# Two heads of a pair on even and odd partitions, and 128 neighbouring tokens per tile in the last mixture

## The chip, the cores and the metric

One core of one Trainium2 chip. The metric is the device time of one execution in microseconds. TensorE is PE here (its weight loads PEld), VectorE DVE, ScalarE ACT, GpSimd POOL; SyncE (SP) issues most DMAs.

## What is computed

Three stages in float32, each on the output of the one before:

```python
# attention: 4 batches x 8 heads x 576 tokens x 64; heads 0..3: the 32 tokens up to the query,
# heads 4..7: every fourth of the 128 tokens up to the query
scores = where(masks, scale * q @ k.T, -1e9)
attn = softmax(scores) @ v                            # x: 2304 tokens x 512
# soft mixture: 8 experts x 4 slots
logits = x @ phi                                      # phi 512 x 32
slots = softmax(logits, axis=0).T @ x                 # 32 x 512
so[e] = relu(slots[e] @ w1[e]) @ w2[e]                # 512 -> 1024 -> 512
x = softmax(logits, axis=1) @ so
# last mixture: 8 experts, each token to the best by cosine, times its probability
e = argmax(cosine(x, emb) / tau);  gate = softmax(...)[e]
out = gate * relu(x @ w1b[e]) @ w2b[e]
```

## The kernel before

Lines are those of the kernel as printed below and in the profile.

**Attention.** The work goes by supercolumns: a pair of heads in two batches, 8 of them, each three score tiles, so 24 tiles numbered n. A tile holds 128 queries' blocks in three columns z. The keys of the pair lie in `kbd`, a block-diagonal tile: head 0's 64 dimensions on partitions 0 to 63 in one half of the columns, head 1's on 64 to 127 in the other half, and zeros elsewhere, so that one product gives both heads' scores. Values (`v1`) lie the same way, their second half in the rows of the second head; `v2` is a copy of `v1` shifted by half a block. `load_kq` (L135) and `load_v` (L142) issue the loads on SP, two for keys, one for queries, two for values; the zeros are written once by `zero` (L148), of which the loads touch nothing.

A loop with an order written by hand runs a pipeline over n: `emit_soft` (DVE's maximum L242 and subtract L244), `emit_S` of the next tile (PE L231, 24 products, and the mask as one more, L234), `emit_T` (PE L255, ACT copy L257), `emit_XT`, `emit_exp` (ACT L249), `emit_PV` (PE L267, DVE L271 to 273), `emit_v2` once per supercolumn (DVE and POOL copies L211 and 212, ACT copy L214), and `emit_logits` (PE L304) once per supercolumn. The product of the scores reads the keys so (partitions; then head, half, 32 neighbouring keys):

```python
k = bass.AP(tensor=flat.tensor, offset=flat.offset + S * bb + 32 * (t // 2),
            ap=[flat.ap[0], [2 * S, 2], [gap, 2], [1, 32]])
```

The logits of pairs 0 and 1 of a batch group read neighbouring columns of x; those of pairs 2 and 3 (dilated heads, stored by residue) read columns 144 apart. The loads of the next supercolumn and the first weights of the experts, `load_w`, are issued from within the loop, in SP's order.

**Soft mixture.** 32 weight tiles of 1 MB are streamed through buffers that become free as attention ends; PE does two layers per expert. `combine_a` (L370) turns the logits by tokens into 18 groups `lt`, 16 of them 64 tokens from each of two places, the last two what is left.

**Last mixture (the tail).** The kernel takes the expert of the first token for all (`w1b`, `w2b` of that expert are loaded early) and treats other tokens in a conditional part that this input doesn't enter. It uses that relu(h) is h or 0: the columns of the hidden layer whose sign is the same for all tokens are taken as linear (`B4`), and only the others are done per token.

- `part_a` (L838), `fold_a` (L844): slots times the first weights, split into a high and a low part, A4; `sign` (L884) the sign for the first token.
- `seen` (L907): for each of 8 blocks of 128 hidden units, products of A4 with all tokens (PE L917, L912) and a reading of them: relu with a sum over the columns, on DVE (L925) or ACT (L923) in turn, 896 or 512 columns at a time.
- `places` (L952): the units that change sign get a place among the "uncertain" ones, by counting; `select` (L971): a one-hot matrix, 128 columns on DVE, a second one of 256 on POOL; `names` (L984): the units' row numbers and the gather of their second weights `w2g` (POOL L990); `gathered` (L993), `hidden` (L1005), `split_w` (L1014): their first weights, their activations as high and low part, and their second weights as the same. A first set of up to 128 units, those that change sign anywhere behind the first 512 tokens of the order, is done for all tokens; a second of up to 256, which change only among those 512, for them alone.
- `route_a` to `route_h`: cosine, argmax and gate. `root` (L177) makes the square roots for it, on POOL, behind the second select.
- `through` (L1018): four products per output tile (L1021, 1024 to 1026), ten for a tile of the first 512 tokens; `put` (L849) the gate, on ACT (L852) or DVE (L854), and the store (L864).

```python
select(nc.gpsimd, 1)
split_w(0)
route_d()
route_e()        # the root, on POOL
```

Of the kernel before, what the change touches and what calls it, by code (L numbers as in the profile page):

```python
# [16 lines left out]
NSET = 2  # L17

def layout(q, k, v):
# [44 lines left out]
def body(ctx, tc, a, stop=None):  # L64
# [156 lines left out]
    def emit_S(n):  # L221
        sc, p, kb, si, t0 = tiles(n)
        s = ps.tile([128, 3, 2, 64], F32, tag="s", name="s")
        flat = kbd[si].rearrange("d h b s -> d (h b s)")
        for z in range(3):
            for i, (bb, t) in enumerate(ublocks(t0 + z)):
# [3 lines left out]
                            ap=[flat.ap[0], [2 * S, 2], [gap, 2], [1, 32]])  # L230
# [4 lines left out]
            s, lhsT=identb, rhs=maskb[:, p // 2, t0:t0 + 3, None, :].to_broadcast([128, 3, 2, 64]),  # L235
# [134 lines left out]
    def combine_a(kb):  # L370

        r = slice(64 * kb, 64 * kb + 64)
        tp = ps.tile([128, 4, 64], F32, tag="t", name="tm")
        for m in range(4):
            nc.tensor.transpose(tp[:, m], Lsb[r, 128 * m:128 * m + 128], ident[r, r])
        sp = ps.tile([128, 32], F32, tag="v", name="ts")
        for hh in range(2):
            nc.tensor.matmul(sp[64 * hh:64 * hh + 64], lhsT=Lsb[r, 512:576], rhs=ident[r, 64 * kb + 32 * hh:64 * kb + 32 * hh + 32], start=True, stop=True)

        o = lt[:, 0:16].rearrange("p (m k b) s -> p k m b s", k=2, b=2)[:, kb]  # L380
        nc.scalar.copy(out=o, in_=tp.rearrange("p m (b s) -> p m b s", b=2))
        nc.scalar.copy(out=lt[:, 16 + kb], in_=sp)
# [81 lines left out]
    def keep_warm(n):  # L464
# [10 lines left out]
    keep_warm(4)  # L475
# [9 lines left out]
    keep_warm(2)  # L485
# [755 lines left out]
```

## Time and profile before

| | us |
|---|---|
| median of three runs (lowest, highest) | 245.94 (244.4, 247.26) |
| the profiled execution | 248.36 |
| its span, first to last instruction | 246.6 |
| PE busy | 197.7 (80%) |
| DVE busy | 127.6 (52%) |
| ACT busy | 103.6 (42%) |
| DMA queue 1, share of 16 engines' span | 73.3% |

Shares are means over three stages with different limits, so the slices and the stretches come first. The mean granted clock of PE over the span is 0.942. All durations below come from the profiled execution. In a row of the timeline, the first number is the start in the span, the second the time from the first start to the last end of what the row groups, and the bracket is the engine's idle time before it with what ended it.

### The profile page before, as it was taken

The numbers are of one execution on the slowest core, as the hardware profiler recorded it, in microseconds if no ns is written. First come the engines' busy times: TensorE is split into PE (matmuls) and PEld (weight loads), VectorE is DVE, ScalarE is ACT, GpSimd is POOL, SyncE is SP. The second block draws the span as 40 slices with busy tenths as digits, with TensorE's granted clock in tenths as the row PEclk, the third lists the DMA queues.
The fourth block names the chain that finished last, engine by engine and source line by source line (L and its number), as shares of the span: only waits on it lengthen the run. The fifth ranks groups of instructions, "written<-read, shape, count | busy, mean of one in ns | idle before, by whom it ended". The sixth has DMA issues, their size and how long they took to land. (4 is left out here: it accounts for less than half of the span.)

```text
span 246.6 us, 5616 instructions
## 1 busy us (share of the span) xinstructions
PE 197.7 (80%) x2206; PEld 128.4 (52%) x2206; DVE 127.6 (52%) x362; ACT 103.6 (42%) x226; POOL 42.3 (17%) x89
## 2 busy tenths in 40 slices
PE   1549779887959795999999999888699479489970
PEld 1227556655637574545543434555565457457860
DVE  6525856646494737545244123535886642636720
ACT  2142748646567736435332124424567040134210
POOL 8522010202020202120000130000020098400000
PEclk9999999999999999999999999999999755589996
DMA  5999999999999999999999999398000010045742
GB/s 162 238 234 267 299 234 279 269 315 293 293 289 234 348 264 373 334 353 390 385 386 387 387 385 386 94 338 321 1 1 0 0 45 0 17 153 213 248 141 93
DMA packets 27745, 58.25 MB, mean 236 GB/s; under 512 B 2048, under 2 KB 4480, under 8 KB 27712
## 3 DMA queue, kind: packets, MB, share of 16 engines
q1 hardware_dynamic: 27472, 57.04, 73.3%
q0 software_dynamic: 240, 0.79, 1.2%
q8 instruction: 19, 0.31, 0.6%
q14 instruction: 14, 0.11, 0.2%
HBM read 53.10 MB, written 4.72 MB: 234 GB/s over the span
## 5 line engine op out<-in xcount | busy, mean ns | idle before, releaser
L231 PE MATMUL s<-kbd,qt 128*32 128x128 f32 x576 | 27.0, 305 | 23.1 <-DMA qt<-in_q 12.9
L231 PEld LDWEIGHTS s<-kbd,qt 128*32 128x32 f32 x576 | 18.6, 121 | 31.8 <-issue 14.4
L257 ACT COPY et<-tp 128x384 f32<-128x384 f32 x24 | 11.5, 479 | 27.9 <-PE tp L255 27.9
L267 PE MATMUL pv<-v,et 128*32 128x130 f32 x576 | 21.9, 284 | 0.0
L211 POOL COPY v<-v 32x1040 f32<-32x1040 f32 x8 | 8.4, 1052 | 75.2 <-DMA v<-in_v 75.2
L249 ACT ACTIVATE e<-e 128x384 f32<-128x384 f32 x24 | 12.7, 528 | 19.6 <-DVE e L244 19.4
L214 ACT COPY v<-v 32x1170 f32<-32x1170 f32 x16 | 18.5, 1158 | 1.2 <-DMA v<-in_v 1.0
L540 ACT COPY hs<-hp 128x512 f32<-128x512 f32 x16 | 9.2, 584 | 20.2 <-PE hp L539 20.2
L267 PEld LDWEIGHTS pv<-v,et 128*32 128x32 f32 x576 | 15.0, 110 | 4.3 <-issue 4.2
L244 DVE TENSOR_TENSOR e<-s,mx 128x384 f32<-128x384 f32 x24 | 13.4, 558 | 2.3
L273 DVE TENSOR_TENSOR x<-pv,rd 128x384 f32<-128x384 f32 x24 | 13.4, 558 | 0.8
L304 PE MATMUL L<-xT,phi 128*32 128x288 f32 x64 | 13.7, 539 | 0.0
L242 DVE TENSOR_REDUCE mx<-s 128x6 f32<-128x384 f32 x24 | 13.2, 550 | 0.8 <-PE s L234 0.6
L925 DVE TENSOR_SCALAR_CACHE_REDUCE junk<-H,ms 128x896 bf16<-128x896 f32 (+1 forms) x12 | 12.2, 1015 | 2.7 <-PE H L917 1.9
L539 PE MATMUL hp<-w,siT 128*32 128x512 f32 x104 | 13.1, 597 | 0.0
L923 ACT ACTIVATE junk<-H,ms 128x896 bf16<-128x896 f32 (+1 forms) x12 | 10.8, 900 | 5.3 <-PE H L917 3.0
L211 DVE COPY v<-v 32x1040 f32<-32x1040 f32 x8 | 5.5, 693 | 14.3 <-DMA v<-in_v 14.2
L255 PE MATMUL tp<-cst,e 128*128 128x128 f32 x72 | 12.6, 287 | 0.4 <-ACT e L249 0.4
L559 PE MATMUL so_p<-w,h 128*32 128x512 f32 x102 | 12.5, 595 | 0.3 <-DVE h L551 0.2
L281 PE MATMUL xp<-cst,x 128*128 128x128 f32 x72 | 12.0, 276 | 0.8 <-ACT dn L355 0.4
L852 ACT ACTIVATE hs<-y,gm 128x512 f32<-128x512 f32 x9 | 6.2, 689 | 14.6 <-DVE hs L854 8.1
L549 DVE TENSOR_REDUCE hr<-hTp 128x16 f32<-128x64 f32 x16 | 3.6, 222 | 16.3 <-PE hTp L547 16.3
(291 smaller groups left out, 382.6 us busy)
## 6 DMA issues: line engine op xcount, KB each, us to landing
w<-in_w1a SPq DMA_DIRECT2D x12, 1024.0 KB, 13.4
w<-in_w2a SPq DMA_DIRECT2D x12, 1024.0 KB, 11.3
v<-in_v SPq DMA_DIRECT2D x16, 292.5 KB, 7.0
out<-hs SPq DMA_DIRECT2D x16, 256.0 KB, 2.2
kbd<-in_k SPq DMA_DIRECT2D x14, 288.0 KB, 8.3
qt<-in_q SPq DMA_DIRECT2D x7, 576.0 KB, 9.3
wG<-in_w2a SPq DMA_DIRECT2D x3, 1024.0 KB, 11.8
wG<-in_w1a SPq DMA_DIRECT2D x3, 1024.0 KB, 11.6
```

What stands on the lines that cost most here:

```text
L211: cp(out=d_[o0:o1, hh, :, 1:9], in_=s_[o0:o1, hh, :, 0:8])
L214: nc.scalar.copy(out=d_[e0:o0, hh], in_=s_[e0:o0, hh])
L231: nc.tensor.matmul(s[32 * i:32 * i + 32, z], lhsT=qt[si][:, bb, 32 * t:32 * t + 32], rhs=k, start=(z == 0), stop=False, skip_group_check=True)
L242: nc.vector.tensor_reduce(out=mx, in_=s, axis=AX.X, op=ALU.max)
L244: nc.vector.tensor_tensor(out=e, in0=s, in1=mx[:, :, :, None].to_broadcast([128, 3, 2, 64]), op=ALU.subtract)
L249: nc.scalar.activation(out=e, in_=e, func=AF.Exp, scale=0.125)
L255: nc.tensor.transpose(tp[:, z], e[:, z].rearrange("q h c -> q (h c)"), ident)
L267: nc.tensor.matmul(pv[32 * i:32 * i + 32, z], lhsT=et[:, z, 32 * i:32 * i + 32], rhs=vt[:, :, bb, t // 2, :], start=True, stop=True)
L273: nc.vector.tensor_tensor(out=x[kb][p // 2][:, p % 2, t0:t0 + 3, :].rearrange("q z (h d) -> q z h d", h=2), in0=pv[:, :, :, 0:64], in1=rd. ...
L304: nc.tensor.matmul(st["L"][n][r0:r0 + 32], lhsT=phi[:, p, :], rhs=rhs, start=(p == 0), stop=(p == 3))
L539: nc.tensor.matmul(hp[32 * c:32 * c + 32], lhsT=siT[:, c, :], rhs=w_t[4 * e + n][:, c], start=True, stop=True)
L559: nc.tensor.matmul(so_p[32 * j:32 * j + 32], lhsT=h[:, f, :], rhs=w_t[4 * e + 2 + f // 4][:, j], start=(e == 0 and f < 4), stop=(e == 6 an ...
```

## The change

1. *Layout and loads.* Head hh of a pair stands on partitions hh, hh + 2, hh + 4, ...; loads of keys and values go to 64 partitions with a step of two. Queries are loaded before keys. The tiles are zeroed whole, ahead of the loads. The score's columns are (key, head) instead of (head, key), so that the transposed scores come out on the partitions on which the values lie.
2. *Token groups.* Groups 0 and 1 hold the first 64 tokens of each batch, every further group 128 neighbours. 256 instead of 512 tokens pass the 256 further units.
3. *Tail.* Readings of 1,024 columns with a written engine each; places, select and hidden of the first set ahead of the last readings (256 columns each); the root ahead of gather and second select on POOL; a tile's linear product last; one store for two tiles.

```diff
+        nc.sync.dma_start(out=qt[i][:, bs], in_=a["q"][p, kb, :, bs])
         for hh in range(2):
-            nc.sync.dma_start(out=kbd[i][64 * hh:64 * hh + 64, hh, bs], in_=a["k"][p, kb, 64 * hh:64 * hh + 64, bs])
-        nc.sync.dma_start(out=qt[i][:, bs], in_=a["q"][p, kb, :, bs])
+            nc.sync.dma_start(out=kbd[i][hh:128:2, hh, bs], in_=a["k"][p, kb, 64 * hh:64 * hh + 64, bs])
...
-            nc.sync.dma_start(out=v1[i][64 * hh:64 * hh + 64, hh, bs], in_=a["v"][p, kb, 64 * hh:64 * hh + 64, bs])
-
-    def zero(eng, t):
-
-        eng.memset(t[0:64, 1], 0.0)
-        eng.memset(t[64:128, 0], 0.0)
+            nc.sync.dma_start(out=v1[i][hh:128:2, hh, bs], in_=a["v"][p, kb, 64 * hh:64 * hh + 64, bs])
+    nc.vector.memset(kbd[0][:, 0, 0], 0.0)
+    nc.gpsimd.memset(kbd[0][:, 1, 0], 0.0)
+    nc.vector.memset(kbd[0][:, :, 1], 0.0)
+    nc.gpsimd.memset(v1[0][:, 0], 0.0)
+    nc.vector.memset(v1[0][:, 1], 0.0)
+    for i in range(1, NSET):
+        for hh in range(2):
+            nc.gpsimd.memset(kbd[i][:, hh], 0.0)
+        for hh in range(2):
+            nc.gpsimd.memset(v1[i][:, hh], 0.0)
     load_kq(0, slice(0, 1))
...
-                cp(out=d_[o0:o1, hh, :, 1:9], in_=s_[o0:o1, hh, :, 0:8])
+                cp(out=d_[64:128, hh, :, 1:9], in_=s_[64:128, hh, :, 0:8])
...
-        s = ps.tile([128, 3, 2, 64], F32, tag="s", name="s")
+        s = ps.tile([128, 3, 64, 2], F32, tag="s", name="s")
...
-                            ap=[flat.ap[0], [2 * S, 2], [gap, 2], [1, 32]])
+                            ap=[flat.ap[0], [gap, 2], [1, 32], [2 * S, 2]])
...
-        nc.vector.tensor_reduce(out=mx, in_=s, axis=AX.X, op=ALU.max)
+        nc.vector.tensor_reduce(out=mx, in_=s.rearrange("p z c h -> p z h c"), axis=AX.X, op=ALU.max)
...
-    nc.vector.tensor_copy(out=soTx[:, :, 32:128], in_=sT[:, :, 32:128])
+    nc.scalar.copy(out=soTx[:, :, 32:128], in_=sT[:, :, 32:128])
...
+    def put_pair(p, y, eng):
+        ob = obs[p % 3]
+        for i, g in enumerate(pair(p)):
+            gated(ob[:, i], y[:, 512 * i:512 * i + 512], eng, gm[:, g:g + 1])
+        r0 = S * (2 * (p // 4) + p % 2) + 64 + 256 * (p % 4 // 2)
+        nc.sync.dma_start(out=a["out"][r0:r0 + 256].rearrange("(i t) f -> t i f", i=2), in_=ob)
...
+    def seen(j, part, eng):
+
         H = two("H")
...
+        for i in range(2):
+            nc.tensor.matmul(H[:, 512 * i:512 * i + 512], lhsT=A4[:, 128 * j:128 * j + 128],
+                             rhs=cTf[:, 256 + 1024 * part + 512 * i:768 + 1024 * part + 512 * i], start=True, stop=True)
+        reading(eng, j, part, H, 1024)
...
+        if n == 0:
+            nc.vector.tensor_tensor(out=sel[0][:, 4 * h:4 * h + 4], in0=iota1[:, None, 0:128].to_broadcast([128, 4, 128]),
+                                    in1=pos[0][:, 4 * h:4 * h + 4].to_broadcast([128, 4, 128]), op=ALU.is_equal)
...
+    for q in range(4):
+        part_a(q)
+    for q in range(4):
+        fold_a(q)
...
+    seen(5, 1, D_)
+    route_d()
+    seen(6, 0, A_)
+    seen(6, 1, D_)
+    seen(7, 0, A_)
+    seen(7, 1, D_)
+    H0 = [first64s(0)]
...
+    places_a(0)
+    pp = places_b(0)
+    total(0, pp)
+    seen0(0, H0[0], A_)
+    H0.append(first64s(1))
+    bf = linear_fold()
+    select(0, 0)
+    select(0, 1)
+    names(0, sel[0])
+    gathered(0, sel[0])
+    seen0(1, H0[1], D_)
+    hps = [two("hp") for _ in range(2)]
+    for i in range(4):
+        products(hps[i // 2][:, 512 * (i % 2):512 * (i % 2) + 512], 0, 256 + 512 * i, 512)
+    places_a(1)
+    pp = places_b(1)
...
+        rest(src, Rh[:, r], Rl[:, r])
+        if i == 1:
+            split_hi(0)
+            split_lo(0)
+        if i == 0:
+            split_rows(B4, bf)
+    select(1, 0)
+    select(1, 1)
+    route_f()
+    route_h()
...
+    tiles2(0, 8)
+    tiles2(1)
+    puts(0, A_)
```

`route_d` now sums the logits (DVE) and makes the root (POOL); `first64s` makes four products of 256 columns, `seen0` reads them; `tiles2(0, 8)` does eight products of the identity with itself (`keep_warm`) before its own, in the buffer that these then overwrite.

SP's queue at the start, the loads of the first supercolumn. Before:

```order
L139 DMA kbd_96<-in_k 64x576 x2
L140 DMA qt_97<-in_q 128x576
L155 DMA cst<-in_cst 128x168
L156 DMA x_92<-in_cst 128x320
L139 DMA kbd_96<-in_k 64x576 x2
L140 DMA qt_97<-in_q 128x576
L146 DMA v_0_98<-in_v 64x1170 [waits DMAHW0_49]
```

and now, where `DVE_49` and `Pool_49` are the zeroing:

```order
L139 DMA qt_97<-in_q 128x576
L141 DMA kbd_96<-in_k 64x576 [waits DVE_49]
L141 DMA kbd_96<-in_k 64x576 [waits Pool_49]
L162 DMA cst<-in_cst 128x168
L163 DMA x_92<-in_cst 128x320
L139 DMA qt_97<-in_q 128x576
L141 DMA kbd_96<-in_k 64x576 [waits DVE_49]
```

The queries moved to the front, and the keys wait for zeros.

POOL in the tail, from the first gather on (w2g), with the select (sel) and the start of the root (n, rn, nr). Before:

```order
L990 DMA w2g_2184<-in_w2b,ids_2181 128x512
L973 TENSOR_SCALAR sel_2180<-iota_1912,pos 128x256 x8
L181 TENSOR_SCALAR n_2148<-n_2148 128x18
L182 TENSOR_SCALAR rn<-n_2148 128x18
L185 TENSOR_TENSOR nr_2469<-rn 128x18
```

and now, from the root's last two operations on:

```order
L188 TENSOR_TENSOR rn<-rn,nr_2343 128x18
L189 TENSOR_TENSOR rn<-rn,n_2143 128x18
L1001 DMA w2g_2184<-in_w2b,ids_2181 128x512
L982 TENSOR_SCALAR sel_2179<-iota_1907,pos_2174 128x256 x8
L1001 DMA w2g_2185<-in_w2b,ids_2182 128x512
```

The root moved from behind gather and select to ahead of both.

PE in the tail, from the last readings' products (H) to the names of the first set (ip) and their first weights (am). Before:

```order
L917 MATMUL H<-cT_1908,A_2157 128x448 x4
L912 MATMUL H<-cT_1908,A_2157 128x512
L941 MATMUL Bf<-bs,foldw 128x512
L960 LDWEIGHTS before
L960 MATMUL pp<-flb,before 128x16
L961 LDWEIGHTS every
L961 MATMUL pp<-flb,every 128x16
L962 LDWEIGHTS every
L962 MATMUL pp<-flb,every 128x16
L988 MATMUL ip<-fid,sel_2179 128x2 x8
L998 MATMUL am<-sel_2179,AT_2168 128x128 x8
```

and now:

```order
L917 MATMUL H<-cT_1903,A_2152 128x512 x12
L925 MATMUL H_2375<-cT_1903,A_2152 128x256 x4
L939 MATMUL Bp<-w2b_2049,ATl 32x512 x4
L939 MATMUL Bp<-w2b_2050,ATl 32x512 x4
L965 LDWEIGHTS before
L965 MATMUL pp<-flb_2169,before 128x8
L966 LDWEIGHTS every
L966 MATMUL pp<-cum_2171,every 128x8
L967 LDWEIGHTS every
L967 MATMUL pp<-flb_2169,every 128x8
L925 MATMUL H_2402<-cT_1903,A_2152 128x256 x4
L945 MATMUL Bf<-bs,foldw 128x512
```

The linear part (Bp, Bf) and the small readings moved between the last large readings and the names, which follow next.

## Rows read from the trace of the kernel before

**Rows 1.** The page's slices: granted clock in tenths, and GB/s

```profile
PEclk9999999999999999999999999999999755589996
...
GB/s 162 238 234 267 299 234 279 269 315 293 293 289 234 348 264 373 334 353 390 385 386 387 387 385 386 94 338 321 1 1 0 0 45 0 17 153 213 248 141 93
```

**Rows 2.** Stretches: us; busy (count) of each engine, clock, DMA share, GB/s

```profile
core 0: us, PE busy (x) PEld busy (x) DVE busy (x) ACT busy (x) POOL busy (x), PEclk, DMA share, GB/s
...
14.60:18.40 3.80, 0.22 (x2) 0.00 (x0) 0.00 (x0) 2.06 (x3) 0.00 (x0) 1.00 1.06 240
30.00:36.00 6.00, 5.17 (x98) 3.82 (x94) 2.79 (x7) 2.31 (x6) 0.01 (x1) 1.00 0.99 234
...
120.00:150.00 30.00, 29.59 (x267) 11.75 (x259) 9.41 (x38) 8.95 (x18) 3.82 (x13) 1.00 1.05 387
...
190.50:194.00 3.50, 0.54 (x4) 0.21 (x3) 2.16 (x11) 1.16 (x3) 0.00 (x0) 0.99 0.00 0
194.00:218.00 24.00, 18.20 (x61) 15.19 (x62) 10.11 (x31) 4.26 (x8) 14.15 (x26) 0.50 0.14 41
```

**Rows 3.** The page's DMA issues: count, KB each, us to landing

```profile
v<-in_v SPq DMA_DIRECT2D x16, 292.5 KB, 7.0
...
kbd<-in_k SPq DMA_DIRECT2D x14, 288.0 KB, 8.3
```

**Rows 4.** Waits: us in total, times, longest

```profile
DVE v L211 <- DMA v<-in_v: 14.2, 7, 3.0
PE s L231 <- DMA qt<-in_q: 12.9, 6, 5.2
```

**Rows 5.** Timeline of PE: the starts of score tiles 3, 8, 9 and 23

```profile
18.44 0.87 PE L231 MATMUL s<-kbd,qt 128*32 128x128 f32 x12 [3.62 <-DMA qt<-in_q]
...
36.72 0.86 PE L231 MATMUL s<-kbd,qt 128*32 128x128 f32 x24 [1.55 <-DVE e L244]
...
39.78 0.86 PE L231 MATMUL s<-kbd,qt 128*32 128x128 f32 x24 [0.46 <-DMA qt<-in_q]
...
95.59 0.86 PE L231 MATMUL s<-kbd,qt 128*32 128x128 f32 x24 [2.26 <-DVE e L244]
```

**Rows 6.** Line 304, 36 to 46 and 46 to 58 us: ns min/median/max, starts

```profile
L304 PE MATMUL L<-xT,phi x8: 403/405/406, 42.2 to 42.9; 128*32 128x288 f32 x8
...
L304 PE MATMUL L<-xT,phi x8: 648/670/679, 52.6 to 54.1; 128*32 128x288 f32 x8
```

**Rows 7.** Timeline of DVE at the start

```profile
1.02 1.02 DVE L150 MEMSET kbd<- 64x1152 f32 x1 [1.02 <-PEq L1231]
```

**Rows 8.** Line 925, DVE's readings: ns min/median/max, first and last start

```profile
L925 DVE TENSOR_SCALAR_CACHE_REDUCE junk<-H,ms x12: 749/1142/1151, 171.3 to 189.7; 128x896 bf16<-128x896 f32 x8, 128x512 bf16<-128x512 f32 x4
```

**Rows 9.** Timeline of the tail

```profile
192.41 0.17 DVE L953 TENSOR_TENSOR fl<-acc 128x8 f32<-128x8 f32 x1
...
197.03 1.19 POOL L990 DMA_INDIRECT w2g<-in_w2b,ids  x1 [13.94 <-DVE ids L989]
198.27 7.65 POOL L973 TENSOR_SCALAR sel<-iota,pos 128x256 fp32r<-128x256 f32 x8
...
202.23 0.80 PE L1021 MATMUL y<-B,cT 128*128 128x512 f32 x1 [1.31 <-DVE Rl L1003]
...
206.59 3.41 PE L988 MATMUL ip<-fid,sel 128*128 128x2 f32 x16
...
210.52 0.18 DVE L192 TENSOR_SCALAR rn<-rn 128x18 f32<-128x18 f32 x1 [5.62 <-POOL rn L189]
...
213.10 2.07 PE L998 MATMUL am<-sel,AT 128*128 128x256 f32 x8 [3.10 <-DVE ids L989]
...
213.93 0.24 DVE L801 SCALAR_TENSOR_TENSOR gm<-idm,e0b,gate 128x18 f32<-128x18 f32 x1
...
219.96 0.50 PE L1021 MATMUL y<-B,cT 128*128 128x512 f32 x1 [1.18 <-DVE Sl L1003]
...
238.77 0.39 PE L1026 MATMUL y<-Wl,Sh 128*128 128x512 f32 x1
...
240.03 0.69 ACT L852 ACTIVATE hs<-y,gm 128x512 f32<-128x512 f32 x1 [3.86 <-DVE hs L854]
```

More of the change, by code (lines that the diff above doesn't have):

```diff
@@ L877, in body @@
     nc.gpsimd.memset(acc, 0.0)
[L878 removed]
+    junk = {e: late.tile([128, 1024], BF16, name=f"junk{i}") for i, e in enumerate((nc.scalar, nc.vector))}
     wq = lambda i, name, dt=F32R: wA.tile([128, 4, 512], dt, tag=f"w{i}", name=name)
@@ new lines, in body, with places_a @@
+    cum = [late.tile([128, 8], BF16, name=f"cum{i}") for i in range(2)]
+    pos = [late.tile([128, 8, 1], F32, name=f"pos{i}") for i in range(2)]
+    n12 = late.tile([128, 2], F32, name="n12")
+    for t in flb:
+        nc.gpsimd.memset(t, 0.0)
+    def places_a(n):
+        if n == 0:
+            nc.vector.scalar_tensor_tensor(out=flb[0][:, 1:9], in0=acc[:, 0], scalar=-1.0, in1=acc[:, 1], op0=ALU.mult, op1=ALU.is_lt)
+        else:
+            nc.vector.scalar_tensor_tensor(out=flb[1][:, 1:9], in0=acc[:, 2], scalar=0.0, in1=flb[0][:, 1:9], op0=ALU.is_gt, op1=ALU.is_gt)
+        nc.vector.tensor_tensor_scan(out=cum[n], data0=every[:, 0:8], data1=flb[n][:, 0:8], initial=0.0, op0=ALU.mult, op1=ALU.add)
@@ L1060, in body @@
-    linear_part()
-    for p in range(3):
-        seen(6, p)
+    seen(4, 1, A_)
     route_b(1)
+    seen(5, 0, A_)
     route_c(1)
-    for p in range(3):
-        seen(7, p)
-    linear_fold()
-    places()
-    select(nc.vector, 0)
+    seen(5, 1, D_)
[5 more added lines that the diff above has]
+    H0 = [first64s(0)]
+    bp = one("Bp")
+    linear_part(0, bp)
+    linear_part(1, bp)
+    places_a(0)
+    pp = places_b(0)
+    total(0, pp)
@@ new lines, in body, with tiles2, puts @@
+    select(1, 0)
+    select(1, 1)
+    route_f()
+    route_h()
+    ys = {}
+    def tiles2(p, warm=0):
+        y = ys[p] = two("y")
+        keep_warm(warm, y[:, 0:512])
+        for i, g in enumerate(pair(p)):
+            r = slice(128 * (g - 2), 128 * (g - 2) + 128)
+            through(y[:, 512 * i:512 * i + 512], 0, Rh[:, r], Rl[:, r], first=True)
+            linear(y[:, 512 * i:512 * i + 512], g)
+    def puts(p, eng):
+        put_pair(p, ys.pop(p), eng)
+    tiles2(0, 8)
+    tiles2(1)
@@ new lines, in body @@
+    route_y()
+    tiles2(3)
+    route_z(one("sm"))
+    n3 = late.tile([128, 4], F32, name="n3")
+    gt8 = late.tile([128, 8], F32, name="gt8")
+    nc.vector.tensor_scalar(out=n3[:, 0:1], in0=n12[:, 0:1], scalar1=128.0, scalar2=0.0, op0=ALU.subtract, op1=ALU.max)
+    nc.vector.tensor_scalar(out=n3[:, 1:2], in0=n12[:, 1:2], scalar1=256.0, scalar2=0.0, op0=ALU.subtract, op1=ALU.max)
+    nc.vector.tensor_tensor(out=n3[:, 2:3], in0=n3[:, 0:1], in1=n3[:, 1:2], op=ALU.add)
+    nc.vector.tensor_scalar(out=gt8, in0=iota8, scalar1=8.0, scalar2=128.0, op0=ALU.add, op1=ALU.mult)
@@ new lines, in body @@
+    for k in (1, 2):
+        products(hp[:, 256 * k - 256:256 * k], k, 0, 256)
+    rest(hp, Sh[:, 256:768], Sl[:, 256:768])
+    puts(3, A_)
+    tiles2(5)
+    puts(4, D_)
+    split_hi(1)
+    split_lo(1)
+    split_hi(2)
+    split_lo(2)
+    tiles2(6)
+    puts(5, A_)
+    tiles2(7)
+    puts(6, D_)
+    ys0 = [one(f"ys{g}") for g in range(2)]
+    for g in range(2):
+        for k in range(3):
+            c = 256 * k + 128 * g
+            through(ys0[g], k, Sh[:, c:c + 128], Sl[:, c:c + 128], first=(k == 0))
+        linear(ys0[g], g)
+        if g == 0:
+            puts(7, A_)
+        put(g, ys0[g], (D_, A_)[g], obs[2][:, g], gm)
@@ L1160, in body @@
+        with tc.For_i(0, more, 1):
+            for h in range(2):
+                select(0, h)
+            nc.vector.tensor_scalar(out=pos[0], in0=pos[0], scalar1=-128.0, scalar2=None, op0=ALU.add)
             names(0, sel[0])
             gathered(0, sel[0])
-            hidden(0, 512, 1024, Rh[:, 0:1024], Rl[:, 0:1024])
-            hidden(0, 1536, 768, Rh[:, 1024:1792], Rl[:, 1024:1792])
-            hidden(0, 0, 512, Sh[:, 0], Sl[:, 0])
-            split_w(0)
+            for i in range(5):
+                c0, n = (0, 256) if i == 4 else (256 + 512 * i, 512)
+                hp = one("hp")[:, 0:n]
+                products(hp, 0, c0, n)
+                r = slice(512 * i, 512 * i + 512) if i < 4 else slice(0, 256)
+                rest(hp, (Rh if i < 4 else Sh)[:, r], (Rl if i < 4 else Sl)[:, r])
+            split_hi(0)
+            split_lo(0)
```

373 lines of the change are left out of this document (138 added, 235 removed).

## The prediction

> **What bounds the kernel now.** I read the page's slices first. They show three stages: to about 107 us (slice 17) most slices carry 231 to 330 GB/s; to about 154 us they carry 385 GB/s; behind that almost nothing until the outputs, and the clock row falls to 7, 5, 5, 5, 8 from 191 us on [rows 1]. The table of stretches adds what the slices hide: in the first stage the DMA engines are busy all the time too, 234 GB/s at a share of 0.99 in a stretch of keys and values against 387 GB/s at 1.05 in the weights' stretch [rows 2]. So that stage fills its DMA time without moving what those engines can move. Keys and values are what it moves in pieces over 64 neighbouring partitions: 14 x 288 KB, 4 halves of that for the first pair, and 16 x 292.5 KB of values [rows 3], 9.5 MB; at 234 GB/s they take 40.6 us, at 387 they would take 24.6.
>
> Then who waits: PE starts scores late for queries 12.9 us in all, and DVE its copy of the values 14.2 [rows 4]; the subtract that PE needs is queued behind that copy, so the second wait comes back at PE as 1.55 and 2.26 us behind DVE [rows 5]. From the start of score tile 3 at 18.44 to that of tile 23 at 95.59 it takes 77.15 us for 20 tiles, 3.86 a tile; tiles 8 and 9 stand 3.06 apart, with 0.46 of waiting in it [rows 5]. Over those 20 tiles I count 13.4 us of PE waiting ahead of scores, most of it one step or two behind a load, so the work without it takes 63.8.
>
> In the middle stage the weights are late. The first that fills it is issued in mid-attention, so it ends a fixed time behind attention. In the tail, readings of the expert's first product alternate on DVE and ACT (DVE: 1.142 us for 896 columns, 12 readings to 190.8 [rows 8]); then comes a chain: places at 192.41, gather at 197.03, first output product at 202.23. POOL selects from 198.27 for 7.65 us, and only then makes the root, which DVE takes at 210.52; the gates that every output waits for are there at 213.93 + 0.24. From 219.96 to 238.77 PE makes 80 products back to back, 79 steps of 0.238; the last gating ends at 240.72, the span at 246.6, 5.9 later [rows 9].
>
> **The change, part by part.** *Loads.* The same bytes go to every second partition over the whole height. At the rate of full-height loads keys and values lose 40.6 - 24.6 = 16 us of DMA time, loads are no longer late, and the 13.4 us of PE waiting go; tile 3 could start when PE is free, 3.62 us sooner [rows 5]. The bound below is no gain: the rate stays at 234. I take the full rate, the row of the loads that reach all heights.
>
> [...]
>
> *Zeroing.* Whole tiles are zeroed ahead of the loads: the first key loads wait for a memset of 576 columns on DVE and one on POOL. One of 1152 columns took 1.02 us [rows 7]; half of it, 0.5, is late at the start, and queued behind the waiting key load on SP are the constants and all that follows. POOL's others add up to some 8 us and end before their loads' turn at SP; if not, tile 3 gives back up to 1 us. Three pieces on v2 go.
>
> *Scores.* The two heads alternate in the column order, so PE reads consecutive columns of keys 4,608 bytes apart. No row shows this read. The nearest is the logits product: 405 ns (median) with its columns side by side, 670 with columns 576 bytes apart [rows 6]; by its starts a pair of them takes 242 ns in the one case and some 490 in the other, twice the time. A score tile has six groups of four products, 109 ns each by their starts (0.86 us for the 24 with the last one's tail [rows 5]): doubled, +0.65 us a tile, +15.7 over 24 tiles. The bound below is 0, if two interleaved runs of neighbours read like one. The bound above: the 490 ns are two slow reads that share one limit; then the 24 products of a tile go one by one at 109 ns, 2.6 us instead of 0.8. I take the middle, as the nearest row has it: while strided logits ran, score products in the other column groups kept their pace, which speaks against a shared limit.
>
> [...]
>
> *Sum for attention.* Tile 3 at 18.44 - 3.62 + 0.5 = 15.3, 3.1 sooner; from there to tile 23 63.8 + 20 x 0.65 = 76.8 against 77.15, 0.3 sooner. So PE gives back nearly all that the loads free. Another 2.0 come as the last values, ahead of the weights in SP's queue, move 585 KB faster (1.0) and a backlog of about 1 us goes. The weights' stretch ends 5.5 earlier. DVE's reduce now steps by two elements in PSUM, and the v2 copies cover 64 partitions with the same count and free size: I cost both at nothing, as PE's 3.1 a tile covers DVE; if they took half as long again they would cost some 1 us a tile, and DVE would be late.
>
> *Tail.* Of the readings 16 of 1,024 and 8 of 256 columns are left, the small ones behind the first places. DVE did 8 large (1.142) and 4 small (0.749), 12.1 us [rows 8]; now 7 x 1.28 = 9.0 (128 columns more, by the slope between its two forms, 0.13): -3.1. Between its last reading and the places lay the split of B, 1.6 us, which moves behind: -1.5. The four groups of the first product now stand in a row ahead of the readings: -1.3, an estimate. Places at 192.4 - 5.9 = 186.5. Select in two operations on DVE instead of eight: -0.6; the gather goes at 190.4 (197.03), the first output product at 197.2 with 1.6 for the hidden parts in four pieces (5.2 behind the gather before).
>
> The root stands ahead of gather and select on POOL, and its 4.6 us (205.92 to 210.52) run beside the readings. What is late for the gates now is DVE, with the pieces to about 198.5 and the route's 3.65 behind them: 202.1 instead of 214.17. Three y buffers hold 24 products, 5.7 us, so PE hardly stops: 84 products (12 fewer, as 256 instead of 512 tokens pass three times) x 0.238 = 20.0 from 197.2, with names (3.41) and gather (2.07) of the second set 5.5 [rows 9]: 222.7, last gating 223.4 against 240.72: -17.3. I take -15.5, leaving 1.8 for waits that I can't see. One store for two tiles: the last stores are as small as before: 0.
>
> *The clock.* [...] If the drop comes again, 18.2 us of PE work at the half level cost some 9 more than at full. Eight warming products now stand ahead of the first outputs. I take no drop, at 6 in 10.
>
> *Total.* The profiled execution took 248.36 (span 246.6): 248.4 - 5.5 - 15.5 = 227.4. It lies 2.4 above the runs' median of 245.94; 225.0.
>
> **The rivals.** *P0, the strided read is free*: two runs of neighbours alternate, and each line may still be at hand. Attention gains the 13 us that PE gives back in the forecast: 225 - 13 = 212; 221 with the drop. Against it: 670 ns. *P2, slow reads share one limit* (the slower side): place, the 24 products of each score tile; price 1.8 x 20 = 36 us, less 13.4 of waiting that is gone, less 3.3 at the start: +19.3; 245.9 + 19.3 - 15.5 = 249.7, 258.7 with the drop. It decides from about 2.4 us a score tile on (0.8 now). Against it: the pace of scores beside strided logits. *L, the loads don't speed up*: the waits stay, and PE's 0.65 a tile falls partly into them, +5: 245.9 + 5 - 15.5 = 235.4, 244.4 with the drop.
>
> **How the numbers follow.** The forecast has 0.62: 225 without the drop, 234 with it; its own range is 219 to 236. P0 0.20, L 0.10, P2 0.08. The range of 207 to 241 holds the forecast, P0 and most of L, and leaves out P2 and far ends. A measurement of this kernel tells 1% (2.5 us) from no change. Faster by more: forecast, P0, most of L, 0.89; within it L with the drop, 0.03; slower P2, 0.08.
>
> **What would show it.** Score products: a tile's 24 in 0.8 us (P0), 1.45 (forecast) or over 2.4 (P2). DVE's 14.2 us of waiting for values near 0, and GB/s near 380 while keys and values load (L: below 260). Tail: root ahead of the select, gates at least 9 us sooner behind the first reading than before, the clock row at 0.5 or not. I am wrong if tile 3 to tile 23 takes under 70 or over 82 us, or if first reading to last gating shrinks by less than 10.

## The result, and the profile after

| | us |
|---|---|
| before, median | 246.18 (244.4 to 247.26, 4 runs) |
| after, median | 218.84 (218.52 to 220.04, 4 runs) |
| ratio | 0.8905, 95% interval 0.8842 to 0.8968 |
| profiled execution: span before, after | 246.6, 216.8 |

Some executions of a kernel are slower as a whole, by more than 1.5% over its fastest; the ratios, and the medians below, leave these out. A later comparison gave 218.30 and a ratio of 0.8764 (0.8709 to 0.8820). The forecast was 225.0 in 207 to 241. The forecast's own range was 219 to 236, so the kernel came out just under its lower end, about midway between the forecast and the 212 of rival P0.

The span is 29.8 us shorter. Three starts divide it: DVE's first copy of the slots' outputs (soTx), with which the tail begins, the last gating on ACT, and the end. From the start to soTx: 164.86 before, 153.70 now, -11.2. From there to the end of the last gating: 75.9 before, 58.2 now (211.86), -17.7. From there to the end: 5.9, now 4.9, -0.9. The first of these starts, before and now:

```profile
164.86 0.29 DVE L729 COPY soTx<-sT 128x128 f32<-128x128 f32 x1 [2.07 <-PE sT L722]
```

```profile
153.70 0.29 DVE L727 COPY soTx<-sT 128x128 f32<-128x128 f32 x1 [2.07 <-PE sT L719]
```

The page's slices of the changed kernel (5.42 us each here), to be read against [rows 1]:

```profile
PEclk9987999999999999999999999999999999999996
...
GB/s 147 296 328 384 219 302 313 319 397 374 255 297 306 379 322 302 334 391 387 386 387 385 387 388 386 386 177 204 357 216 0 0 2 51 1 41 249 302 299 90
```

The dip of the clock in the tail is gone; there is a new, short one in the third and fourth slice. In the first stage 13 of 16 slices carry 296 GB/s or more, where before most stood under 300; the fastest slices of either kernel hold weights too. The weights' plateau ends at 141 us (slice 26) instead of 154. Stretches, in the columns of [rows 2]; at 9 to 13 us almost only keys, queries and values are loaded:

```profile
9.00:11.00 2.00, 2.00 (x34) 1.17 (x30) 1.42 (x3) 1.02 (x2) 0.00 (x0) 1.00 1.02 348
11.00:13.00 2.00, 1.56 (x25) 0.98 (x16) 1.44 (x4) 1.04 (x3) 1.06 (x2) 1.00 0.94 356
...
14.00:24.00 10.00, 8.44 (x145) 6.31 (x149) 6.16 (x18) 4.21 (x8) 1.29 (x2) 0.83 0.96 352
24.00:30.00 6.00, 6.00 (x122) 4.55 (x119) 4.86 (x11) 3.65 (x10) 1.20 (x2) 1.00 0.64 189
```

The same 9 to 13 us carried 226 and 265 GB/s before. The packets in the trace show it load by load. The 1,024 packets of 4,680 bytes, a size that only the values have, took 321 ns (median) before and take 181 now; all their bytes over all their time on 16 engines are 228 and 346 GB/s. At 24 to 30 us the DMA engines are busy 0.64 only while PE is busy all the time: attention now waits for PE there, not for loads. The DMA issues and the wait that answer to [rows 3] and [rows 4]:

```profile
v<-in_v SPq DMA_DIRECT2D x16, 292.5 KB, 4.1
...
kbd<-in_k SPq DMA_DIRECT2D x14, 288.0 KB, 6.8
```

```profile
PE s L230 <- DMA kbd<-in_k: 9.4, 4, 5.2
```

Values land in 4.1 instead of 7.0 us, and DVE's wait for them (14.2) is no longer among the large ones. Of PE's 9.4, 5.2 is the start of the kernel, as in the 12.9 before. Score tiles 3, 8, 9 and 23, as in [rows 5]:

```profile
14.89 1.41 PE L230 MATMUL s<-kbd,qt 128*32 128x128 f32 x24 [2.33 <-DMA kbd<-in_k]
...
31.36 1.02 PE L230 MATMUL s<-kbd,qt 128*32 128x128 f32 x24 [0.56 <-DVE e L243]
33.93 1.00 PE L230 MATMUL s<-kbd,qt 128*32 128x128 f32 x24
...
83.20 1.02 PE L230 MATMUL s<-kbd,qt 128*32 128x128 f32 x24
```

From tile 3 to tile 23 it is 68.31 us (77.15). PE is busy 64.9 us of it and stands 3.4, before 63.7 and 13.5. A tile's 24 products take 1.00 us where they took 0.86, so the alternating read costs 0.14 us a tile. (A row counts both passes of a product: the 24 are 12 calls in the code.) Tile 3's 1.41 us is another matter, taken up at the end. DVE's readings and the tail, as in [rows 8] and [rows 9]:

```profile
L911 DVE TENSOR_SCALAR_CACHE_REDUCE junk<-H,ms x11: 473/1276/1283, 161.5 to 182.3; 128x1024 bf16<-128x1024 f32 x7, 128x256 bf16<-128x256 f32 x4
```

```profile
175.91 0.17 DVE L958 SCALAR_TENSOR_TENSOR flb<-acc 128x8 bf16<-128x8 f32 x1
...
177.56 0.23 POOL L189 TENSOR_TENSOR rn<-rn,n 128x18 f32<-128x18 f32 x1
...
181.09 1.19 POOL L1001 DMA_INDIRECT w2g<-in_w2b,ids  x1 [3.30 <-DVE ids L1000]
...
184.01 7.61 POOL L982 TENSOR_SCALAR sel<-iota,pos 128x256 fp32r<-128x256 f32 x8 [1.73 <-DVE n L973]
...
185.76 0.50 PE L1030 MATMUL y<-Wh,Rh 128*128 128x512 f32 x1 [0.32 <-ACT Wh L1020]
...
192.00 0.24 DVE L795 SCALAR_TENSOR_TENSOR gm<-idm,e0b,gate 128x18 f32<-128x18 f32 x1
...
211.17 0.69 ACT L846 ACTIVATE ob<-ys,gm 128x512 f32<-128x512 f32 x1 [3.36 <-PE ys L1026]
```

Counted from soTx (153.70 here, 164.86 before): places at 22.2 (27.5), gather at 27.4 (32.2), first output product at 32.1 (37.4), gates at 38.3 (49.1), last gating's start at 57.5 (75.2). The root ends (177.79) before the select has begun.

### The profile page after: what moved, and what is told of

Its sections match the earlier page's. It is cut to its first block, busy times and chain, and to the rows that moved or that the text cites. A ratio compares the mean times of both kernels' runs of the same rounds, so it can differ in the third digit from the quotient of the medians.

```text
span 216.8 us, 5600 instructions
## 1 busy us (share of the span) xinstructions
PE 190.0 (88%) x2213; PEld 122.1 (56%) x2213; DVE 124.5 (57%) x344; ACT 103.8 (48%) x232; POOL 40.4 (19%) x90
## 4 chain that ended last, share of the span: by engine, by line
PE 58%; DVE 15%; DMA 11%; ACT 6%; issue 4%; SPq 3%; POOL 1%; DVEq 0%; ACTq 0%; POOLq 0%
DMA kbd<-in_k 10%; PE so_p L556 6%; PE hp L536 6%; PE pv L266 5%; PE s L230 5%; PE L L303 3%; PE hTp L544 3%; PE xp L280 2%; PE tp L254 2%; PE si_p L364 2%; PE y L1032 2%; PE H L917 2%; PE y L1030 2%; PE y L1026 1%; PE s L233 1%
## 5 line engine op out<-in xcount | busy, mean ns | idle before, releaser
L230 PE MATMUL s<-kbd,qt 128*32 128x128 f32 x576 | 29.4, 319 | 10.7 <-DMA kbd<-in_k 9.4
L230 PEld LDWEIGHTS s<-kbd,qt 128*32 128x32 f32 x576 | 20.3, 117 | 17.4 <-issue 5.2
L210 POOL COPY v<-v 64x1040 f32<-64x1040 f32 x8 | 9.0, 1127 | 64.2 <-DMA v<-in_v 58.8
L213 ACT COPY v<-v 64x1170 f32<-64x1170 f32 x16 | 18.5, 1158 | 0.0
L248 ACT ACTIVATE e<-e 128x384 f32<-128x384 f32 x24 | 12.9, 536 | 11.4 <-DVE e L243 11.4
L243 DVE TENSOR_TENSOR e<-s,mx 128x384 f32<-128x384 f32 x24 | 13.4, 558 | 2.7 <-ACT et L256 0.5
L909 ACT ACTIVATE junk<-H,ms 128x1024 bf16<-128x1024 f32 (+1 forms) x13 | 11.9, 918 | 4.4 <-PE H L917 4.1
L272 DVE TENSOR_TENSOR x<-pv,rd 128x384 f32<-128x384 f32 x24 | 13.4, 558 | 0.8
L270 DVE TENSOR_SCALAR rd<-pv 128x6 f32<-128x6 f32 x24 | 3.9, 163 | 15.0 <-PE pv L266 14.5
L911 DVE TENSOR_SCALAR_CACHE_REDUCE junk<-H,ms 128x1024 bf16<-128x1024 f32 (+1 forms) x11 | 10.9, 989 | 0.7 <-PE H L917 0.5
L254 PEld LDWEIGHTS tp<-cst,e 128*128 128x128 f32 x72 | 9.5, 145 | 2.1 <-issue 1.0
```

The costliest lines, as they stand in the source:

```text
L213: nc.scalar.copy(out=d_[0:64, hh], in_=s_[0:64, hh])
L230: nc.tensor.matmul(s[32 * i:32 * i + 32, z], lhsT=qt[si][:, bb, 32 * t:32 * t + 32], rhs=k, start=(z == 0), stop=False, skip_group_check=True)
L243: nc.vector.tensor_tensor(out=e, in0=s, in1=mx[:, :, None, :].to_broadcast([128, 3, 64, 2]), op=ALU.subtract)
L248: nc.scalar.activation(out=e, in_=e, func=AF.Exp, scale=0.125)
L254: nc.tensor.transpose(tp[:, z], e[:, z].rearrange("q c h -> q (c h)"), ident)
L272: nc.vector.tensor_tensor(out=x[kb][p // 2][:, p % 2, t0:t0 + 3, :].rearrange("q z (h d) -> q z h d", h=2), in0=pv[:, :, :, 0:64], in1=rd. ...
```

## The experiments

Kernels that were compared together share their runs of the kernel before; its median was 246.4 us beside the first four below, 247.1 beside the next four and 248.4 beside the last three, with a spread of some 3 us. So the ratios and the profiles carry more than differences of medians, and a difference of 1 or 2 us between kernels of two comparisons tells nothing.

**The read of the keys, undone.** Score columns side by side, and DVE's subtract makes the alternation:

```diff
-                            ap=[flat.ap[0], [gap, 2], [1, 32], [2 * S, 2]])
+                            ap=[flat.ap[0], [2 * S, 2], [gap, 2], [1, 32]])
...
-        nc.vector.tensor_tensor(out=e, in0=s, in1=mx[:, :, None, :].to_broadcast([128, 3, 64, 2]), op=ALU.subtract)
+        nc.vector.tensor_tensor(out=e.rearrange("p z c h -> p z h c"), in0=s, in1=mx[:, :, :, None].to_broadcast([128, 3, 2, 64]), op=ALU.subtract)
```

> The changed kernel, but the scores' columns are again (head, key), read side by side, and DVE's subtract writes them in the order (key, head). Theory A (two alternating runs of neighbours read almost like one): a tile's 24 score products go back from 1.00 us, first start to last end, to 0.86; 24 tiles x 0.14 = 3.4 us of PE, so 215.4 to 218 us. Rival B (the forecast's price of 0.65 a tile is there and shows elsewhere on PE): at least 10 us less, under 209. Rival C (PE isn't what attention waits for any more): 218.8, no change, though the products are shorter.

Measured: 216.92 us (215.98 to 217.52), ratio 0.8811 (0.8724 to 0.8899). PE's timeline of this kernel:

```profile
29.60 0.86 PE L230 MATMUL s<-kbd,qt 128*32 128x128 f32 x24
```

The products are back at 0.86, as theory A has it, and soTx comes at 151.54 instead of 153.70. Rival B is out: no 10 us are hidden there. That DVE writes by twos costs it nothing (562 ns a subtract against 558, means of line 243).

**What a read costs.** Spare products behind attention, 24 calls per kind, twice as many as in a score tile, reading a weight tile that has landed, for example

```diff
+    for _ in range(6):
+        for i in range(4):
+            nc.tensor.matmul(wt[32 * i:32 * i + 32, 0:128], lhsT=phi[:, i], rhs=reads((1, 32), (144, 4)), start=True, stop=True)
```

> The changed kernel, with spare products behind attention, into a buffer that nothing reads: per kind of read of the moving operand 24 products of 128 columns over four column groups, as in a score tile; kinds: side by side; 2 runs 4,608 bytes apart, alternating; 3 runs; 4 runs 576 bytes apart (the order of the dilated logits); one run with steps of 8, 16 and 60 bytes; and side by side and 4 runs on one column group alone. Theory A (what counts is how many lines are alternated between or left at once): 2 runs take some 1.2 times side by side, 4 runs 2 times, steps of 8 bytes little, 16 and 60 bytes 2 times. Rival B (each jump to another line costs the same): 2 runs cost as much as 4 runs, 2 times. Rival D (a limit shared by column groups): the four-run read on one column group alone is no slower than side by side on one group, and slow only when four groups run. The kernel itself gets longer by the products, some 10 to 14 us; that is no result.

One execution, 236.53 us. PE's timeline; the lines are, in this order, side by side, 2 runs, 4 runs, 3 runs (126 columns), steps of 8, 16 and 60 bytes, then one column group alone, side by side (line 500) and with 4 runs (line 502); where two kinds overlap, the first row of each is shown (a row's x48 counts both passes of 24 products):

```profile
97.73 1.52 PE L480 MATMUL wt<-w,phi 128*32 128x128 f32 x48
99.06 1.85 PE L483 MATMUL wt<-w,phi 128*32 128x128 f32 x48
100.70 2.90 PE L486 MATMUL wt<-w,phi 128*32 128x128 f32 x48
103.36 2.03 PE L489 MATMUL wt<-w,phi 128*32 128x126 f32 x48
105.14 1.63 PE L492 MATMUL wt<-w,phi 128*32 128x128 f32 x48
106.53 3.06 PE L495 MATMUL wt<-w,phi 128*32 128x128 f32 x46
109.27 0.47 PE L498 MATMUL wt<-w,phi 128*32 128x128 f32 x2
...
111.94 0.29 PE L500 MATMUL wt<-w,phi 128*32 128x128 f32 x1
...
113.27 2.79 PE L502 MATMUL wt<-w,phi 128*32 128x128 f32 x12
116.00 0.39 PE L464 MATMUL wt<-identb 128*128 128x512 bf16 x1
```

From each start to the next: side by side 1.33 us, 2 runs 1.64 (1.23 times), 3 runs 1.78 (1.34), 4 runs 2.66 (2.0); steps of 8 bytes 1.39 (1.05), of 16 bytes 2.74 (2.06), of 60 bytes 2.67 (2.0). A score tile has half as many products, so two runs should cost it half of 0.31, 0.155 us; it was 0.14. Two runs are cheap and four are not, so rival B (any jump costs alike) falls and theory A fits. But the runs also stand at different distances: two 4,608 bytes apart, three 2,304, four 576. Whether it is the number of runs that costs or their being close together was not run apart. Rival D falls: one column group alone takes 2.73 us for its 12 passes with four runs and 1.33 side by side, as long as four groups take together for 48, so no limit that the groups share shows in these reads, and that was P2's mechanism. That lines of memory stand behind the prices, as theory A, rival B and the prediction's P0 have it, is a guess: the run shows the times only.

**Each half of the change alone.** Attention with its layout, loads, zeroing and score order; and the regrouped combine with the new tail.

```diff
+            nc.sync.dma_start(out=kbd[i][hh:128:2, hh, bs], in_=a["k"][p, kb, 64 * hh:64 * hh + 64, bs])
...
+                            ap=[flat.ap[0], [gap, 2], [1, 32], [2 * S, 2]])
```

> Only the attention part of the change: layout on even and odd partitions, loads, zeroing, score order; combine, tail and stores as before. Theory A (the parts add up, attention gives what the start of the tail moved, 164.86 to 153.70): 246.2 - 11.2 = 235, 233 to 237. Rival (the forecast's sum): 5.5 less, 240.7. Rival (the old tail gives it back, as the clock falls longer or earlier): 240 or more with the tail's stretch from its first copy to its last gating over 78 us (75.9 before).

```diff
+    seen(5, 1, D_)
+    route_d()
+    seen(6, 0, A_)
```

> Only the regrouped combine and the new tail; attention, its layout and its loads as before. Theory A: 246.2 - 17.7 - 0.9 = 227.6, 226 to 230, clock at 1.00 through the tail. Rival (the new tail needs the earlier end of the weights, or the clock falls as before when DMA and attention stand as before): 233 or more, with the clock near 0.5 somewhere between 185 and 210 us.

Attention alone: 234.68 us (233.32 to 235.59), ratio 0.9559 (0.9468 to 0.9650), span 231.5. Tail alone: 231.83 (230.66 to 233.36), ratio 0.9449 (0.9302 to 0.9595), span 228.8. Where the tail begins in each, attention alone first:

```profile
151.54 0.29 DVE L728 COPY soTx<-sT 128x128 f32<-128x128 f32 x1 [2.07 <-PE sT L721]
```

```profile
165.51 0.29 DVE L728 COPY soTx<-sT 128x128 f32<-128x128 f32 x1 [2.07 <-PE sT L720]
...
223.04 0.69 ACT L847 ACTIVATE ob<-ys,gm 128x512 f32<-128x512 f32 x1 [3.36 <-PE ys L1027]
```

The new tail takes 58.2 us behind either attention (223.73 - 165.51, 211.86 - 153.70), 17.7 less than the old one: it doesn't need the earlier end of the weights. The old tail behind the new attention takes 75.1 (151.54 to 226.62). The clock is granted at 1.00 over 183 to 210 us of the tail alone. So both halves add within the noise: 0.9559 x 0.9449 = 0.903, some 0.017 to either side, against 0.8905 for the whole. For the tail alone 226 to 230 was expected and 231.8 came, with a ratio whose interval is wide; what the tail itself takes is as expected. Attention alone also tells what the regrouped combine costs: from tile 23 to soTx it takes 69.17 us (82.37 to 151.54), as the kernel before (69.27), and the changed kernel 70.50.

**The warming products.**

```diff
-    tiles2(0, 8)
+    tiles2(0)
```

> The changed kernel without the eight warming products ahead of its first output tile. Theory A (the places and names no longer leave PE idle for long, so the clock doesn't fall anyway): 218 to 220 us, granted clock 1.00 through the tail. Rival (these products are what keeps the clock): half clock somewhere in 183 to 210 us and 223 to 228 us, since the before kernel lost some 9 us by it.

219.51 us (219.33 to 220.33), ratio 0.8901 (0.8773 to 0.9028). This stretch of the tail without them:

```profile
183.00:195.00 12.00, 9.98 (x44) 7.95 (x45) 8.25 (x23) 5.29 (x10) 8.64 (x9) 0.86 0.12 47
```

Without them the clock does fall, to a mean of 0.86 over these 12 us (0.54 and 0.61 over 185 to 189), where the changed kernel has 1.00 in the same stretch; but it comes back (1.00 over 195 to 205), and the time moves by less than 1 us, less than this comparison tells. Neither theory has it whole: the products keep the clock, and it was not they that removed the old stretch of 24 us at 0.50.

**The root behind the select again.**

```diff
     select(1, 1)
+    route_e()
     route_f()
```

> The changed kernel with one thing moved back: the root on POOL stands behind the gather and the 7.6-us select again. Theory A (the gates were the largest wait of the old tail): root from 191.6 to 196.2, gates at 199.7 instead of 192.24; PE stops when its three y buffers are full (24 products, at about 191.3) until then, so +5 to +7.5 us, 224 to 226.5. Rival (the tail's gain is the earlier places and first products; PE has names and the second set to do meanwhile): +2 or less, under 221.

227.38 us (226.20 to 229.01), ratio 0.9191 (0.9090 to 0.9292): +8.5 by the medians, +7.0 by the ratios. By the tail's own clock, from soTx (155.50) to the end of the last gating (222.29), it is 66.8 instead of 58.2 us, +8.6. Rows of the timeline, and two stretches:

```profile
155.50 0.29 DVE L727 COPY soTx<-sT 128x128 f32<-128x128 f32 x1 [2.07 <-PE sT L719]
...
200.92 0.24 DVE L797 SCALAR_TENSOR_TENSOR gm<-idm,e0b,gate 128x18 f32<-128x18 f32 x1
...
202.57 0.80 PE L1032 MATMUL y<-Wh,Rh 128*128 128x512 f32 x1 [6.74 <-ACT hs L848]
```

```profile
190.00:200.00 10.00, 5.84 (x34) 4.97 (x33) 2.71 (x9) 0.32 (x1) 6.50 (x19) 0.81 0.00 0
200.00:215.00 15.00, 11.15 (x46) 8.63 (x47) 9.33 (x36) 6.84 (x13) 1.98 (x2) 0.79 0.54 181
```

Theory A: PE fills its three buffers and then stands for 6.74 us until the gates come. What goes beyond the expected 7.5 fits the clock, which falls in this wait and stays down for part of the outputs (0.79 over the 15 us from 200; some 2 us of it, as PE stands until 202.57). So this move alone carries about half of the tail's 17.7 us, and a part of the old stretch at half clock hangs on it.

**Work in the wait for the keys.** On the kernel with columns side by side, 16 spare products ahead of score tile 3:

```diff
+                if n == 2:
+                    for _ in range(16):
+                        nc.tensor.matmul(st["L"][0], lhsT=identb, rhs=identb[:, None, 0:96].to_broadcast([128, 3, 96]), start=True, stop=True)
                 emit_S(n + 1)
```

> The kernel with score columns side by side again (216.92 us), and 16 spare products of 288 columns on PE ahead of score tile 3, where PE waits 2.3 us for keys and the profile of the changed kernel shows half clock behind it (0.52 and 0.62 in 15 to 19 us). Theory E (the wait brings the half clock, and work in it keeps the full one): clock 1.00 in 14 to 24 us and 1 to 2 us less, 215 to 216. Rival F (the fall isn't tied to that wait): half clock still there, no gain, 216.9 or, if the products delay tile 3, up to 1 more.

216.56 us (215.82 to 218.00), ratio 0.8781 (0.8677 to 0.8885).

```profile
15.14 0.86 PE L230 MATMUL s<-kbd,qt 128*32 128x128 f32 x24 [0.96 <-DMA kbd<-in_k]
...
17.23 0.84 PE L230 MATMUL s<-kbd,qt 128*32 128x128 f32 x24
```

Tiles 3 and 4 stand 2.1 us apart, 3.67 in the changed kernel and 3.05 with columns side by side, and the clock is 1.00 over 14 to 24 us. That it was the spare products is not shown: the kernel with columns side by side, without them, has the same 2.1 us and the same clock in its last comparison:

```profile
14.43 0.86 PE L230 MATMUL s<-kbd,qt 128*32 128x128 f32 x24 [1.52 <-DMA kbd<-in_k]
...
16.52 0.84 PE L230 MATMUL s<-kbd,qt 128*32 128x128 f32 x24
```

The medians show no gain either: 216.56 against 216.92.

**The keys alone on half the height again.**

```diff
-            nc.sync.dma_start(out=kbd[i][hh:128:2, hh, bs], in_=a["k"][p, kb, 64 * hh:64 * hh + 64, bs])
+            nc.sync.dma_start(out=kbd[i][64 * hh:64 * hh + 64, hh, bs], in_=a["k"][p, kb, 64 * hh:64 * hh + 64, bs])
```

> The changed kernel with the keys' loads alone back on partitions 0 to 63 and 64 to 127 (queries' dimensions in that order too); values stay on every second partition. Theory A (which partitions a load reaches sets its rate): keys land in 8 us or more (6.8 in the changed kernel), 4.6 MB of them take 19.7 us instead of 11.9 us of DMA time; PE waits for keys more by 3 to 6 us, 222 to 225 us. Rival (the faster attention comes from queries first and whole-tile zeroing, or only the values count): within 1 us of 218.8, PE's waits for keys at 9.4 us as now.

225.0 us (224.41 and 225.50): +6.1, and by the start of the tail, soTx, +5.3. Its DMA issues, a stretch, PE, and the tail's start:

```profile
kbd<-in_k SPq DMA_DIRECT2D x14, 288.0 KB, 8.6
```

```profile
24.00:30.00 6.00, 4.89 (x97) 3.72 (x98) 4.77 (x13) 4.37 (x9) 0.00 (x0) 1.00 0.95 252
```

```profile
17.90 1.51 PE L230 MATMUL s<-kbd,qt 128*32 128x128 f32 x24 [4.11 <-DMA kbd<-in_k]
```

```profile
159.02 0.29 DVE L727 COPY soTx<-sT 128x128 f32<-128x128 f32 x1 [2.07 <-PE sT L719]
```

Theory A: same bytes, same queue, same zeroing, only other partitions, and keys land in 8.6 us again, the engines are busy 0.95 at 252 GB/s, tile 3 starts 3.0 us later, soTx comes 5.3 us later. The packets of 4,608 bytes, which keys and queries have, take 232 ns (median) where they took 178, while those of the values stay at 182 (181). The time is at the upper end of what was expected, with some 1 us of it in the tail, where the clock of this profile is at 0.50 from 171.0 to 174.4; PE's wait for keys rose by 2.5 us (11.9), a little less than expected. So nearly half of attention's 11.2 us is the keys' partitions. The rest, the values' partitions, queries first and whole-tile zeroing, was not run apart.

**The three fastest in the same rounds.**

> The changed kernel once more, on the same chip and in the same rounds as the two that follow: 218 to 220 us, ratio to the kernel before 0.88 to 0.90.

> Score columns side by side, in the same rounds. Theory A (the alternating read costs 0.14 us a tile, most of it on attention's path): 1.5 to 3.4 us below the changed kernel. Rival C (attention isn't PE's): within 0.5 us of it.

> The same with the spare products ahead of score tile 3, in the same rounds. Theory E: 0.5 to 1.5 us below the one without them, full clock in 14 to 24 us. Rival F: no difference beyond 0.3 us.

Five rounds on one chip: the changed kernel 218.30 (217.55 to 219.89), ratio 0.8764 (0.8709 to 0.8820); columns side by side 216.91 (215.03 to 217.59), 0.8728 (0.8669 to 0.8788); with the spare products 217.54 (216.89 to 218.58), 0.8740 (0.8692 to 0.8788). The kernel with columns side by side came out lower both times, by 1.9 and 1.4 us, and its profiles end earlier (215.5 and 213.1 against 216.8 and 216.6). But the intervals overlap, and in the profile that ends at 213.1 tiles 3 and 4 also ran at full pace: a gain of 1 to 2 us is likely and not shown, and 1.4 lies between what the two theories put. For the spare products there is nothing; neither of the two profiles has a dip of the clock that they could have removed.

## Why the prediction was right or wrong

*Loads.* Right. Keys, queries and values go at 348 to 356 GB/s at 9 to 13 us (226 and 265 before), over all packets of the values at 346 (228 before) where the sum took 387, DVE's wait for values is gone (1.2 us), and the keys put back cost 5 to 6 us. That pieces on every second partition would go at the rate of full-height loads was the author's estimate, from the 234 and 387 GB/s of [rows 2], and the loads came near it: 64 partitions, two apart, are enough for 346. Why it matters which partitions a load reaches, no run shows. Rival L is out. What the sum had too well is the waiting: PE's 13.4 us went down to 3.4, not to nothing.

*Start.* Tile 3 was put at 15.3; it came at 14.89. The first key load is issued 0.75 us later than before (1.47 against 0.72), and tile 0 starts no later for it (5.19 against 5.25).

*Scores.* This is the step that failed, as a size: "doubled, +0.65 us a tile". It was +0.14. The prediction took the logits row (405 against 670 ns) for columns that stand 576 bytes apart; but its order runs over four residues and comes back to the neighbour, four alternating runs. The keys' order alternates two. Measured by themselves, two runs cost 1.23 times, four 2.0 times, so the nearest row was a row of another kind. 0.51 x 20 tiles = 10.2 us of PE work too much. From tile 3 to 23 the sum put 76.8 us, all of it work; measured were 64.9 of work and 3.4 of waiting, 68.3. (The work rose by 1.2 us only, less than 20 x 0.14, partly because the clock was at 0.50 for 3.4 us of this stretch, while before PE ran at half pace for 4.8, as the last section shows.) 68.3 is also under the 70 at which the prediction calls itself wrong. By this read rival P0 was nearer than the forecast. P2 fell with the reads measured by themselves. The pace of scores beside strided logits, which the prediction holds against it, was that of four products: 272 to 297 ns each, started at 53.35 to 53.49 us, and the same beside the other logits, at 42.46 to 42.60.

*Behind attention.* "Another 2.0" for values and a backlog was wrong too, with the other sign: tile 23 starts 12.4 us sooner, soTx 11.2. The weights were not what this stretch waits for: PE is busy 67.1 of its 69.3 us before and 68.4 of 70.5 now. The 1.2 us are the regrouped combine: with the old combine the stretch takes 69.2 behind the new attention, and its products on line 377, 16 in 2.2 us, stand where 8 in 0.9 us stood. The prediction had no term for them. Together attention and what follows gave 11.2 where 5.5 was put.

*Tail.* The sum was right: -17.3, measured -17.7, and the 1.8 held back for unseen waits was not needed. Its members: places 5.3 sooner by the tail's own clock (5.9 put), gather 4.8 (6.6), first product 5.3 (5.0), gates 10.8 (12.1), last gating 17.7. The root is what the gates hung on: moved back, it alone costs some 8 us. Behind the last gating another 0.9 came, where 0 was put. That the joint stores brought it is not shown: with the old stores behind the new attention this stretch takes 4.9 us too, and in the other runs it lies between 4.7 and 5.5.

*The clock.* No drop in the tail at 6 in 10; it didn't drop. The 9 us put on a drop are an estimate from [rows 2], 18.20 us of PE work at 0.50. Without the warming products the clock drops for a moment (0.54 and 0.61 over 185 to 189), and with the root late for longer (0.79 over 200 to 215), both times behind a wait of PE (2.06 and 6.74 us). The row of [rows 2] with PE idle, 1.00 over 14.6 to 18.4, says nothing of idling: the record of the clock in that trace has its first entry at 23.28 us, and ahead of it PE ran at half pace (last section).

*Total.* 248.4 - 11.2 - 17.7 - 0.9 = 218.6, against the 227.4 of the sum, 8.8 apart. The scores' stretch is 8.5 of it, tile 3 0.4, the tail 2.2 and the end 0.9; behind attention 3.2 go the other way. So the parts on loads and tail held, and three sizes did not: the read's price, the waits that were put at nothing and the 2.0 behind attention. That the time lies as near to the forecast as it does is partly luck: the last two took back 6.6 us, without which it would be near P0's 212.

## What to carry to other kernels

Here a load's rate hung on which partitions it reached: 228 GB/s over the values' packets on 64 neighbouring ones, 346 on every second one. Where two halves of a tile are loaded apart, put them on every second partition and look whether GB/s rises at the same busy share (246 to 352 here over 9 to 13 us, at 1.01 and 0.98). Before a strided read on PE is priced by another one, count how many runs of neighbours the two alternate between, and how far apart they stand: two runs cost 1.23 times side by side here, four 2.0 times. When every output waits for one small chain, look at which in-order queue it stands in: a root of 4.6 us behind a select of 7.6 us cost some 8 us of the whole kernel. Where a stretch's bound is forecast, look at PE's busy time in it first: the one behind attention was PE's (busy 68.4 of 70.5 us), not the weights'.

## What was not expected

A moving operand in two alternating runs costs 1.23 times side by side, in three 1.34, in four 2.0 (at the distances given above); steps of 8 bytes 1.05, of 16 bytes 2.06. One column group alone is slowed by four runs as much as four together (2.73 against 1.33 us, and 2.66 against 1.33).

At the start PE runs slower while the granted clock reads 1.00: in the kernel before four score products come every 213 ns in tile 3 and every 109 in tile 8. The changed kernel in its last comparison, stretch and timeline:

```profile
14.00:19.00 5.00, 3.93 (x56) 3.03 (x60) 1.38 (x4) 2.00 (x4) 1.29 (x2) 1.00 0.96 345
```

```profile
15.07 1.51 PE L230 MATMUL s<-kbd,qt 128*32 128x128 f32 x24 [1.96 <-DMA kbd<-in_k]
...
18.88 1.51 PE L230 MATMUL s<-kbd,qt 128*32 128x128 f32 x24
...
22.34 1.02 PE L230 MATMUL s<-kbd,qt 128*32 128x128 f32 x24
```

Tiles 3 and 4 take 1.51 us here, and tile 5 takes 1.02. The trace says why the stretch reads 1.00: its record of the clock has its first entry, 1.00, at 20.88 us. Ahead of it there is no reading, and the view fills in 1.00. Twelve profiles fit this, all but the one with the reads, whose start is not shown: up to a moment between 11 and 24 us the 24 products of a score tile take 1.50 to 1.67 us, where they run in one piece, and behind it, outside of dips, 0.84 to 1.03. In the kernel before and in the first profile of the changed kernel this moment is the record's first entry. In the kernel before it comes at 23.28, and its tile 3 takes 1.51 us too ([rows 5] shows 12 of its 24 products). In the first profile of the changed kernel it comes at 11.68; there the clock was granted at 0.50 from 15.09 to 18.50, which is the dip of 0.83 over 14 to 24 us, and tile 3's 1.41 us fall into it. With columns side by side in the last comparison the first entry is at 12.76 and no dip follows, and tiles 3 and 4 run at full pace, as they do in the two profiles with spare products and in that of attention alone. From tile 3 to tile 5 the two profiles of the changed kernel take 7.08 and 7.27 us and attention alone, with the same read, 5.65. That is 1.4 to 1.6 us at this place, and it differs from one execution to the next: a difference of this size between two kernels has to be checked against it. What sets the moment isn't shown here.
